# Column-tiled products, padded-query scores, merges by transfer and shift passes on GpSimd in a fused attention and MLP kernel

## The chip, the cores and the metric

The kernel runs on one core of one Trainium2 chip. The metric is the device time of one execution in microseconds (us); the number given for a kernel is the median of its runs, and lower is better. A core has TensorE (PE; its weight loads are listed apart as PEld), VectorE (DVE), ScalarE (ACT), GpSimd (POOL) and SyncE (SP), each with its own instruction queue that it works off in order. They meet through semaphores.

## The reference

```python
def reference(A_x, A_wqkv, A_wo, B_x, B_w1, B_b1, B_w2, B_b2):
    xn = _layernorm(A_x, axis=-1)            # x: [1, 2048, 448] bfloat16
    # A: attention, 16 heads of 28
    qkv = (xn @ wqkv).reshape(B, S, 3, H, Dh).transpose(2, 0, 3, 1, 4)
    scores = jnp.einsum("bhqd,bhkd->bhqk", q, k) * Dh ** -0.5
    p = _softmax(scores, axis=-1)
    s = jnp.einsum("bhqk,bhkd->bhqd", p, v).transpose(0, 2, 1, 3).reshape(B, S, D) @ wo
    # B: two dense layers, hidden width 1792
    h = _gelu(jnp.einsum("bsd,df->bsf", xn, w1) + b1)
    g = _silu(jnp.einsum("bsf,fd->bsd", h, w2) + b2)
    return A_x + s * g
```

Everything is bfloat16 on the outside; products are gathered in float32.

## The kernel before, in words

**Layout.** The 16 heads are 4 groups (g) of 4 heads; a head has a band of 32 partitions, 28 of which are its width. `qT` and `kT` hold queries and keys with the head's width on partitions, `vaug` the values with a column that gives the row sums. The 2048 queries are 4 chunks (c) of 512. A **block** is one group with one chunk, b = 4g + c, 16 in all, and a block has 64 **score tiles** of 128 keys by 512 queries for one head (16 key tiles by 4 heads): 1024 tiles in all. The last block's queries are cut into 256, 128 and 128, so that its end is short.

**Score tiles.** `t_score` (L1605) makes score tiles with matmuls of 32 rows: the four heads of a group lie in the four bands of partitions, so up to four such matmuls run side by side (row form). The result goes to the seven PSUM banks of `ring`. For most tiles ScalarE takes two (or three) banks at a time through Exp (`p_exps`, L1671) into slots `P`, which spill into idle parts of `h` and `xnT`.

**Quads.** Some key tiles are given to VectorE: four tiles of one key tile are a *quad* (`p_late`, `pick`; at most the eight key tiles of `VT` in a block). `p_apass` (L1901) turns a score bank by a scale and an offset into a 16-bit integer whose bits are an approximate exponential in bfloat16. `p_expq` (L1944) then makes two more copies of the whole quad with the integers shifted by `SH[1]` and `SH[2]` (L1960, one VectorE instruction of 128x2048 each), and the sum of the three copies, the shifted ones weighted by `VC` through `vs`, is the exponential. Under a condition (`MG`, `GQ`, `GE`) GpSimd adds the two shifted copies in four instructions of 128x512 (L1973), a *merge*; then the quad needs two products a tile instead of three. The memory for quads is a list of 23 units cut out of tensors that are idle at the time (`unit`, `unit_of`).

**Products with the values.** `t_pv` (L2033) multiplies tiles with `vaug` (or `vs`) in column form: each head writes its own 32 partitions of the PSUM bank `acc`, and four such matmuls run side by side. All other products (`t_proj` for queries and keys, `t_v` for values, `t_f1` and `p_f2` for the dense layers, `t_wo` for the output) are full 128x128 matmuls; the last 32-row pieces of some of them (`rest`) are put among score matmuls in row form.

**Normalising.** When a block is complete, `p_epi` (L2106) copies `acc` to `E_sb` (L2111, VectorE). SyncE writes the row sums to HBM (`sums`, L2117) and reads them back spread over partitions (`rs`, L2119). GpSimd raises them to the power -1 (`rc`, L2121). SyncE writes the reciprocals out (`recs`, L2123) and reads them back broadcast in four transfers (`rb`, a part of `x_sb`, L2126). GpSimd multiplies (L2130) into `qT`, whose queries are no longer needed. `t_wo` (L2140) takes these for the output of a chunk once group 3 is done, and `t_oev` forms s * g + x and stores it, for chunks 0 and 1 by an accumulating transfer from GpSimd's queue (L2166).

**What sets the order.** At build time a planner walks through the work with a clock of its own. Every piece is a `_Task` with an engine, a duration and a latency, and `start_of` (L185) says when it could start: after its inputs, after the engine's earlier work, 0.1 later where TensorE changes its form (`SWITCH`), and, for tasks marked `port`, after VectorE or GpSimd let go of what they share. `run` puts the earliest task next, within `EPS` the one of the lowest priority. What `put` (L207) has written is each engine's queue; the chip then follows it with semaphores alone. A table of knobs `BP` has a row for each block, loaded by `tune` when the scores of that block begin. `NQ` says how many picks of quads a block makes. `K.dma` books transfers with a landing time that the code assumes.

The gelu stretch lies between blocks 8 and 9: ScalarE changes its table, runs the hidden layer through Gelu, 24 of its 56 tiles straight from banks that TensorE fills at that time (`p_direct`), and changes the table back.

Of the kernel before, what the change touches and what calls it, by code (L numbers as in the profile page):

```python
# [6 lines left out]
dt = mybir.dt  # L7
ACTF = mybir.ActivationFunctionType
ALU = mybir.AluOpType
# [7 lines left out]
DH = 28  # L17
F = 1792
G = 4
C = 4  # L20
KT = 4
T = 16
FT = F // 128
# [7 lines left out]
BPN = ('S4', 'QF', 'MG', 'GQ', 'GE', 'EPS', 'HP', 'JIT', 'RM', 'RG', 'WT', 'PV0', 'PVC', 'MP', 'ND4', 'LU', 'JOINT', 'LQ', 'JMAX', 'DQ', 'URG', 'SLACK', 'UR', 'QLEAD', 'QDIST', 'R3')  # L31
BP = (
# [17 lines left out]
)  # L50
NQ = (14, 15, 11, 13, 12, 16, 14, 5, 16, 15, 16, 16, 16, 16, 14, 16)
# [10 lines left out]
MG, GQ, GE = 1, 4.0, 12  # L62
GP, MP4, GL = 4.64, 1, 1.2
# [3 lines left out]
R3 = 0  # L67
# [21 lines left out]
SEM, OWN = 0.07, 0.03  # L89
# [5 lines left out]
EA = 1  # L95
G3P = 0
# [15 lines left out]

class _Task:
    __slots__ = ("E", "fn", "reads", "writes", "dur", "lat", "rank", "w", "mode", "rows", "port")
# [5 lines left out]
    def __init__(self, E, fn, reads=(), writes=(), dur=0.1, lat=0.05, prio=5, w=1.0, mode="full", rows=(), port=False):  # L120
        self.E, self.fn, self.reads, self.writes = E, fn, list(reads), list(writes)
        self.dur, self.lat, self.rank, self.w = dur, lat, prio, w
        self.mode, self.rows, self.port = mode, set(rows), port
        if E == DVE:
            ov = min(OVERLAP, 0.4 * self.dur)
            self.dur, self.lat = self.dur - ov, self.lat + ov


class _Kernel:
    def __init__(self, nc, A_x, A_wqkv, A_wo, B_w1, B_b1, B_w2, B_b2, out):  # L130
# [12 lines left out]
        self.port = {DVE: 0.0, POOL: 0.0}  # L143
        self.procs = []
# [40 lines left out]
    def start_of(self, t):  # L185
# [5 lines left out]
        if t.port:  # L191
            s = max(s, self.port[t.E])
# [7 lines left out]
        for b in t.writes:  # L200
# [3 lines left out]
            s = max(s, b.tr + SEM)  # L204
        return s

    def put(self, t, start=None):  # L207
# [3 lines left out]
        sem = self.evsem[t.E]  # L211
        self.evcnt[t.E] += 1
# [6 lines left out]
        self.prog[t.E].append(lambda eng, f=t.fn, s=sem: f(eng).then_inc(s, 1))  # L219
        h = (sem, self.evcnt[t.E])  # L220
# [11 lines left out]
        if t.port:  # L232
            self.port[DVE if t.E == POOL else POOL] = start + t.dur
        self.tE[t.E] = max(self.tE[t.E], start + t.dur)
# [262 lines left out]
    def alloc(self):  # L497
# [16 lines left out]
        self.P = sb("P", [128, NP, 512], bf)  # L514
        self.E_sb = sb("E_sb", [128, 2, 512], bf)
# [94 lines left out]
        self.b_dum = B()  # L610
        self.b_vs = [[B() for _ in range(NS)] for _ in range(2)]
# [27 lines left out]
        self.s_x0b, self.s_wqk1 = self.sem("s_x0b"), self.sem("s_wqk1")  # L639
        self.s_out = [self.sem("s_out%d" % q) for q in range(14)]  # L640
# [1603 lines left out]
```

## Time and profile before

| | |
|---|---|
| median of 3 runs | 426.8 us (424.96 to 427.39) |
| the profiled execution | 425.0 us span |
| ScalarE | 407.8 us busy, 435 instructions |
| TensorE | 403.8 us busy, 3705 matmuls |
| VectorE | 345.9 us busy, 588 instructions |
| GpSimd | 214.2 us busy, 214 instructions |
| reciprocals on GpSimd (L2121) | 15, 3104 ns mean |
| merges on GpSimd (L1973) | 64 instructions, 1145 to 1601 ns |
| shift passes on VectorE (L1960) | 118, 676 to 1933 ns |
| accumulating transfers (L2166) | 4 of 224 KB, 4.3 us to landing |

A line of the groups gives line, engine, operation, what is written from what, the shapes and the number of instructions; then busy time in us and the mean of one in ns; then the time for which the engine stood idle just before them, and what ended it. A line of the timeline gives start, length, engine, line and operation. Matmuls overlap, so the length of a matmul is not its step: the step is read from one start to the next. A form such as 32*128 is active rows by active columns. In square brackets stands the idle time before, and its releaser.

### The profile page before, as it was taken

The page shows a single profiled execution, that of the slowest core. Times are in us where ns is not written, and L with a number is a line of the kernel's source. Part 1 is how long each engine was busy: PE and PEld are TensorE (multiplying, and loading weights), DVE is VectorE, ACT ScalarE, POOL GpSimd, SP SyncE. Part 2 cuts the span into 40 slices and gives each one's busy share as a digit, 9 for nine tenths or more (in the row PEclk, how much of TensorE's full clock was granted, in tenths as well). Part 3 has the DMA queues.
Part 4 walks back from the last instruction along what each step waited for, and adds up shares of the span by engine and source line. Part 5 has one row for each costly group of instructions (what it writes and reads, how often), then busy time and mean ns, then how long its engine had stood idle before and what let it go on. Part 6 is the DMA issues. An engine that isn't in the chain of part 4 may idle for free.

```text
span 425.0 us, 9807 instructions
## 1 busy us (share of the span) xinstructions
PE 403.8 (95%) x3705; PEld 134.1 (32%) x3705; DVE 345.9 (81%) x588; ACT 407.8 (96%) x435; POOL 214.2 (50%) x214
## 2 busy tenths in 40 slices
PE   6999999999999999999999999999999999999985
PEld 4533222333222222222223442332222233223452
DVE  8969998579989998999975127679789968899865
ACT  6999999999999999999999999999999999999983
POOL 7590330784291405406374324677599678523720
PEclk9999999999999999999999999999999999999998
DMA  8702000010000000100230100001000010206232
GB/s 259 267 3 39 2 27 2 2 26 17 27 1 27 2 25 4 29 2 2 59 122 27 26 0 2 2 3 26 2 3 25 3 28 2 69 3 113 25 73 66
DMA packets 17721, 15.31 MB, mean 36 GB/s; under 512 B 8893, under 2 KB 14761, under 8 KB 17642
## 3 DMA queue, kind: packets, MB, share of 16 engines
q1 hardware_dynamic: 16810, 13.07, 11.3%
q0 software_dynamic: 576, 0.92, 1.7%
q8 instruction: 30, 0.49, 0.5%
q10 hardware_dynamic: 288, 0.69, 0.4%
q14 instruction: 17, 0.14, 0.1%
HBM read 12.60 MB, written 2.94 MB: 37 GB/s over the span
## 4 chain that ended last, share of the span: by engine, by line
PE 66%; DVE 14%; ACT 13%; issue 5%; POOL 1%; POOLq 0%; DVEq 0%; ACTq 0%
PE ring L1617 17%; PE acc L2052 15%; PE ring L1468 9%; PE ring L1537 9%; ACT P L1671 9%; PE ring L1042 5%; ACT h L1671 3%; DVE w L1901 3%; PE ring L2140 2%; PE ring L1438 2%; PE ring L1390 2%; DVE x_sb L1960 2%; PE ring L1058 2%; DVE h L1960 1%; DVE h L1450 1%
## 5 line engine op out<-in xcount | busy, mean ns | idle before, releaser
L1671 ACT ACTIVATE P<-ring 128x1024 bf16<-128x1024 f32 (+1 forms) x262 | 259.2, 1114 | 1.5 <-PE ring L1617 1.1
L1617 PE MATMUL ring<-qT,kT 32*128 32x512 bf16 (+2 forms) x1152 | 148.6, 359 | 6.3 <-ACT P L1671 1.7
L1671 ACT ACTIVATE h<-ring 128x1024 bf16<-128x1024 f32 (+1 forms) x82 | 86.0, 1139 | 2.0 <-PE ring L1617 1.8
L1617 PEld LDWEIGHTS ring<-qT,kT 32*128 32x128 bf16 x1152 | 40.1, 91 | 121.3 <-ACT P L1671 59.8
L2121 POOL TENSOR_TENSOR rc<-rs,mone 128x16 f32<-128x16 bf16 x15 | 46.6, 3104 | 21.5 <-DMA rs<-sums 21.4
L1537 PE MATMUL ring<-w,h 128*128 128x448 bf16 x224 | 55.0, 356 | 0.6 <-ACT xnT L1671 0.5
L1468 PE MATMUL ring<-xnT,w 128*128 128x512 bf16 x201 | 54.3, 382 | 0.8 <-DVE w L1901 0.6
L2052 PE MATMUL acc<-P,vaug 128*32 128x512 bf16 (+2 forms) x627 | 52.8, 354 | 0.0
L1901 DVE TENSOR_SCALAR x_sb<-ring 128x512 uint16<-128x512 f32 x64 | 42.8, 685 | 8.4 <-PE ring L1617 8.0
L1671 ACT ACTIVATE xnT<-ring 128x1024 bf16<-128x1024 f32 (+1 forms) x34 | 35.4, 1119 | 1.6 <-PE ring L1617 1.6
L1901 DVE TENSOR_SCALAR w<-ring 128x512 uint16<-128x512 f32 x52 | 34.4, 684 | 1.0 <-PE ring L1617 0.7
L1901 DVE TENSOR_SCALAR h<-ring 128x512 uint16<-128x512 f32 x40 | 27.0, 686 | 3.7 <-PE ring L1617 3.2
L2130 POOL TENSOR_TENSOR qT<-x_sb,E_sb 128x512 bf16<-128x512 f32 x15 | 18.1, 1209 | 22.8 <-DMA x_sb<-recs 22.6
L1345 POOL TENSOR_TENSOR qsq<-qT 128x512 bf16<-128x512 bf16 x12 | 12.7, 1071 | 32.7 <-DVE qT L1339 31.4
L1468 PEld LDWEIGHTS ring<-xnT,w 128*128 128x128 bf16 x201 | 16.5, 97 | 28.0 <-issue 9.4
L2052 PE MATMUL acc<-h,vaug 128*32 128x512 bf16 x213 | 24.7, 385 | 0.3 <-DVE w L1960 0.2
L1537 PEld LDWEIGHTS ring<-w,h 128*128 128x128 bf16 x224 | 16.1, 97 | 25.8 <-issue 15.5
L1339 DVE CAST qT<-ring 128x512 bf16<-128x512 f32 x15 | 10.3, 686 | 13.2 <-PE ring L1042 13.1
L1985 POOL TENSOR_SCALAR vs<-vaug 128x128 bf16<-128x128 bf16 x32 | 10.2, 320 | 21.0 <-PE acc L2052 10.7
L2052 PEld LDWEIGHTS acc<-P,vaug 128*32 128x32 bf16 x627 | 13.9, 95 | 16.7 <-issue 13.7
L2140 PE MATMUL ring<-wo,qT 128*128 128x448 bf16 x64 | 17.0, 386 | 2.3 <-POOL qT L2130 1.5
L1450 DVE TENSOR_SCALAR h<-ring,b1c 128x512 bf16<-128x512 f32 x23 | 17.0, 744 | 2.4 <-PE ring L1438 1.2
(232 smaller groups left out, 657.0 us busy)
## 6 DMA issues: line engine op xcount, KB each, us to landing
x_sb<-recs SPq DMA_DIRECT2D x60, 64.0 KB, 2.0
w<-in_B_w_dram SPq DMA_DIRECT2D x1, 1568.0 KB, 7.7
w<-in_B_w_dram SPq DMA_DIRECT2D x1, 1344.0 KB, 8.5
x_sb<-in_A_x_dram SPq DMA_DIRECT2D x2, 448.0 KB, 5.6
out_dram<-in_A_x_dram SPq DMA_DIRECT2D x2, 448.0 KB, 10.0
out_dram<-h POOLq DMA_DIRECT2D x4, 224.0 KB, 4.3
out_dram<-h SPq DMA_DIRECT2D x8, 112.0 KB, 1.7
h<-in_A_wqkv_dram SPq DMA_DIRECT2D x3, 168.0 KB, 5.2
```

The lines of the kernel that those rows point to most:

```text
L1042: return eng.matmul(bank, w[:, k, g * 128:(g + 1) * 128], K.xnT[:, k, c * 512:(c + 1) * 512], start=(k == 0), stop=(k > 0), skip_group_che ...
L1450: yield _Task(DVE, lambda eng: eng.tensor_scalar(dst, bank, K.b1c[:, ft:ft + 1], None, op0=ALU.add), [tok, K.b_b1c], wr, 0.69, 0.0, 2)
L1468: return eng.matmul(bank, K.w1[:, k, ft * 128:(ft + 1) * 128], K.xnT[:, k, c * 512:(c + 1) * 512], start=(k == 0), stop=(k > 0), skip_grou ...
L1537: ins = eng.matmul(ps, hv[:, ft, t * 128:(t + 1) * 128], K.w2[:, ft, :], start=(ft == 0), stop=(ft == FT - 1))
L1617: return eng.matmul(dst, K.kT[32 * j:32 * j + 32, g, t * 128:(t + 1) * 128], K.qT[32 * j:32 * j + 32, g, c * 512 + q0:c * 512 + q0 + nq], ...
L1671: return eng.activation(reg[:, i0:i0 + n, :], src, ACTF.Exp, scale=SM_SCALE)
L1901: yield _Task(DVE, lambda eng: eng.tensor_scalar(K.part(u, k).bitcast(dt.uint16), K.like(u, bank), SM_SCALE * LOG2E * 128.0, (127.0 - EXP_ ...
L1960: yield _Task(DVE, lambda eng, W=W, T=T, i=i: eng.tensor_scalar(W.bitcast(u16), T.bitcast(u16), float(SH[i]), None, op0=ALU.add), bT, bW, ...
L2052: return eng.matmul(K.acc[32 * j:32 * j + 32, q0:q0 + nq], w, ap[:, col:col + nq] if len(ap.shape) == 2 else ap[:, col // 128:(col + nq) / ...
L2121: yield _Task(POOL, lambda eng: eng.tensor_tensor(K.rc[:, :], K.rs[:, :], K.mone[:, 0:1].to_broadcast([128, 16]), ALU.pow), [K.b_srs, K.b_ ...
L2130: yield _Task(POOL, lambda eng: eng.tensor_tensor(dst, K.rb, E, ALU.mult), [K.b_rb, tE], [K.b_onT[g][c]], 1.15, 0.05, 1, port=True)
L2140: ins = eng.matmul(ps, K.qT[:, g, c * 512 + t * 128:c * 512 + (t + 1) * 128], K.wo[:, g, :], start=(g == 0), stop=(g == G - 1))
```

## The change

Seven things change. (1) A new helper `_mm` splits a full product into four column tiles of 32 columns; the products of queries, keys, values, both dense layers and the output use it, transposes, first projections and column sums do not. (2) `p_pad` copies one head's queries of a block into `qpad`, a 128-row tensor that is zero elsewhere, and `p_alone` makes single tiles of quads with it in column form, with all 128 rows of `kT`. (3) A merge is one accumulating transfer from GpSimd's queue (512 KB within SBUF) instead of four GpSimd instructions, not for units 16 to 18 and not once the scores have reached block `TXB` = 14; there are 27 of them. (4) GpSimd waits for VectorE's last `port` instruction before one of its own if the planner has them close. (5) In the blocks where `PS` is set (9 and 11), one of the two shift passes of a quad is an int32 add on GpSimd in two halves: 12 passes. (6) From block `RV` = 11 on the reciprocals are taken on VectorE. (7) The table of knobs, which gets five more columns, and `NQ` have new values, and some times that the planner assumes are changed.

```diff
-BPN = (..., 'QLEAD', 'QDIST', 'R3')
+BPN = (..., 'QLEAD', 'QDIST', 'R3', 'CN', 'CS', 'SR', 'PS', 'PQ')
 BP = (
-    (1, 1, 1, 0.383, 11, 0.1, 1.15, -0.216, 0.326, 0.685, 1.08, 13, 3, 2.292, 5, 7, 0.135, 2, 1, 1, 17, 0.325, 0.811, 70, 16, 1),
...
+    (1, 1, 0, 0.383, 15, 0.1, 1.544, -0.216, 0.326, 0.811, 1.017, 13, 3, 2.292, 5, 7, 0.124, 4, 1, 1, 17, 0.367, 0.811, 74, 17, 1, 1, 3.0, 1, 0, 4.0),
...
-NQ = (14, 15, 11, 13, 12, 16, 14, 5, 16, 15, 16, 16, 16, 16, 14, 16)
+NQ = (14, 14, 16, 15, 11, 10, 9, 16, 13, 8, 11, 16, 13, 4, 8, 12)
...
+TXI, TXL = 0.95, 5.3
+CN, CS, SR = 1, 3.0, 1
+PS, PQ, PH, PD = 0, 4.0, 2, 2.3
+TXB = 14
+PJ = 3
...
-SEM, OWN = 0.07, 0.03
+SEM, OWN, SEMW = 0.07, 0.03, 0.15
...
+RV = 11
...
+def _mm(eng, out, w, x, start, stop):
+    ins = None
+    for q in range(0, 128, 32):
+        ins = eng.matmul(out[q:q + 32, :], w[:, q:q + 32], x, tile_position=(0, q), start=start, stop=stop, skip_group_check=True)
+    return ins
...
     def start_of(self, t):
...
         if t.port:
-            s = max(s, self.port[t.E])
+            s = max(s, self.port[t.E] + (SEM if t.E == POOL else 0.0))
...
-            s = max(s, b.tr + SEM)
+            s = max(s, b.tr + (SEMW if t.mode == "row" and t.E == PE else SEM))
...
     def put(self, t, start=None):
...
         self.deps(t.E, t.reads, t.writes)
+        if t.port and t.E == POOL and start < self.port[POOL] + 4.0:
+            self.wait(POOL, self.port_h)
+        sem, by = self.evsem[t.E], 1
+        if t.tx:
+            sem, by = self.s_tx[self.n_tx % len(self.s_tx)], 16
+            self.n_tx += 1
...
     def t_f1(self, c, ft, bank, tok, k, prio=None):
...
-            return eng.matmul(bank, K.w1[:, k, ft * 128:(ft + 1) * 128], K.xnT[:, k, c * 512:(c + 1) * 512],
-                              start=(k == 0), stop=(k > 0), skip_group_check=True)
+            return _mm(eng, bank, K.w1[:, k, ft * 128:(ft + 1) * 128], K.xnT[:, k, c * 512:(c + 1) * 512], k == 0, k > 0)
...
+    def p_pad(self):
+        K = self
+        yield _Task(POOL, lambda eng: eng.memset(K.qpad[:, :], 0.0), [], [K.b_pad], 1.1, 0.05, 2)
...
+        for b in range(1, NBLK - 1):
+            yield ("until", lambda: K.lq_end or len(K.lq) > 0 and K.sub_of(K.lq[0][0]) >= b)
...
+            sl = slice(32 * PJ, 32 * PJ + 32)
+            K.dma(SP, lambda eng, sl=sl, g=g, c=c: eng.dma_start(K.qpad[sl, :], K.qT[sl, g, 512 * c:512 * c + 512]), K.s_pad,
+                  reads=[K.b_qT[g][c]], writes=[K.b_pad], land=max(K.now, K.b_pad.tr, K.b_pad.tw) + (6.0 if b < 3 else 4.5))
+            K.pad_b = b
...
+    def p_alone(self):
...
+            bank, tok = yield ("bank", ok, lambda: CS, 1.0, "col")
+            e = find()
+            m = e[0] + PJ
+            e[2].remove(m)
...
+            yield _Task(PE, lambda eng, g=g, t=t, bank=bank: _mm(eng, bank, K.kT[:, g, 128 * t:128 * t + 128], K.qpad[:, :], True, True),
+                        [K.b_pad, K.b_kT[g][t // 4]], [tok], 0.218, 0.17, CS)
+            K.spawn(K.p_apass(e[1], e[0], PJ, bank, tok), e[0])
...
     def p_expq(self, m0, u):
...
         for i in (1, 2):
             W, T, bW = *K.pair(us[i], u), K.b_U[us[i]]
+            if PS in (i, 3) and K.tE[POOL] < K.now + PQ:
+                n = (W.shape[1] if len(W.shape) == 3 else 1024) // PH
+                for h in range(PH):
...
+                        return eng.tensor_tensor(w, x, k.to_broadcast(list(w.shape)), ALU.add)
+                    q = slice(4 // PH * h, 4 // PH * h + 4 // PH)
+                    yield _Task(POOL, fs, bT[q] + [K.b_shc], bW[q], PD / PH, 0.05, 2, port=True)
...
+                continue
             yield _Task(DVE, lambda eng, W=W, T=T, i=i: eng.tensor_scalar(W.bitcast(u16), T.bitcast(u16), float(SH[i]), None, op0=ALU.add),
                         bT, bW, 0.69, 0.0, 4, port=True)
...
-        if MG and K.next_m < 64 * (m0 // 64 + 1) - GE and K.tE[POOL] < K.now + GQ:
+        if MG and not {16, 17, 18} & set(us[1:]) and K.next_m < min(64 * (m0 // 64 + 1) - GE, 64 * TXB) and K.tE[POOL] < K.now + GQ:
             v, w = us[1:]
-            for k in range(0, 4, MP4):
...
-                yield _Task(POOL, lambda eng, W=W, X=X: eng.tensor_tensor(W, W, X, ALU.add), bs[0] + bs[1], bs[0], GP * MP4 / 4, 0.05 if k + MP4 < 4 else GL, 2, port=True)
+            W, X = K.unit[v], K.unit[w]
+            yield _Task(POOL, lambda eng: eng.dma_start(W, X, accum_op=ALU.add), K.b_U[v] + K.b_U[w], K.b_U[v], TXI, TXL, 2, tx=True)
...
     def p_epi(self, b):
...
-        yield _Task(POOL, lambda eng: eng.tensor_tensor(K.rc[:, :], K.rs[:, :], K.mone[:, 0:1].to_broadcast([128, 16]), ALU.pow),
-                    [K.b_srs, K.b_pads], [K.b_rc], 3.0, 0.05, 1)
+        if b >= RV:
+            yield _Task(DVE, lambda eng: eng.reciprocal(K.rc[:, :], K.rs[:, :]), [K.b_srs], [K.b_rc], 0.2, 0.05, 1)
+        else:
+            yield _Task(POOL, lambda eng: eng.tensor_tensor(K.rc[:, :], K.rs[:, :], K.mone[:, 0:1].to_broadcast([128, 16]), ALU.pow),
+                        [K.b_srs, K.b_pads], [K.b_rc], 3.0, 0.05, 1)
```

More of the change, by code (lines that the diff above doesn't have):

```diff
@@ L514, in alloc @@
         self.P = sb("P", [128, NP, 512], bf)
+        self.qpad = sb("qpad", [128, 512], bf)
+        self.shc = sb("shc", [128, 2], dt.int32)
         self.E_sb = sb("E_sb", [128, 2, 512], bf)
@@ L639, in alloc @@
         self.s_x0b, self.s_wqk1 = self.sem("s_x0b"), self.sem("s_wqk1")
+        self.s_tx, self.n_tx = [self.sem("s_tx%d" % q) for q in range(8)], 0
         self.s_out = [self.sem("s_out%d" % q) for q in range(14)]
@@ L1163, in f @@
                 return ins
-            return _Task(PE, f, [K.b_wqk[which][0], K.b_pads, K.b_xnT[0][k] if h else K.b_x0h[k]], [tok], 0.218, 0.17, which)
+            return _Task(PE, f, [K.b_wqk[which][0], K.b_pads, K.b_xnT[0][k] if h else K.b_x0h[k]], [tok], 0.218, 0.17, which, mode="full")
         def kproj(h):
@@ L1226, in f @@
             for _ in range(3):
-                ins = eng.matmul(K.acc[:, 0:128], K.zero[:, :], K.ident[:, :], start=False, stop=True,
-                                 skip_group_check=True)
+                ins = _mm(eng, K.acc[:, 0:128], K.zero[:, :], K.ident[:, :], False, True)
             return ins
@@ L1249, in f @@
             return ins
-        yield _Task(PE, f, K.b_wsq[g0:g1] + [K.b_pads], [tok], 0.15 * n + 0.1, 0.1, pr, 0.15)
+        yield _Task(PE, f, K.b_wsq[g0:g1] + [K.b_pads], [tok], 0.15 * n + 0.1, 0.1, pr, 0.15, mode="full")
         for b in K.b_hf[1]:
@@ L1351, in p_q @@
         bank2, tok2 = yield ("bank", lambda: K.ready([tq]), pp)
-        yield _Task(PE, lambda eng: eng.matmul(bank2, K.bsel[:, :], qs, start=True, stop=True),
+        yield _Task(PE, lambda eng: _mm(eng, bank2, K.bsel[:, :], qs, True, True),
                     [tq, K.b_bsel], [tok2], 0.216, 0.17, pp if g == 0 else 4)
@@ L1389, in f @@
                     ap = bass.AP(tensor=K.wv, offset=kt * WS + h0 * DH, ap=[[KT * WS, 128], [1, nh * DH]])
-                    ins = eng.matmul(bank[:, off:off + nh * DH], K.xnT[:, kt, t * 128:(t + 1) * 128], ap,
-                                     start=(kt == 0), stop=(kt > 0), skip_group_check=True)
+                    ins = _mm(eng, bank[:, off:off + nh * DH], K.xnT[:, kt, t * 128:(t + 1) * 128], ap, kt == 0, kt > 0)
             return ins
@@ L1536, in f @@
                 for ft in (2 * q, 2 * q + 1):
-                    ins = eng.matmul(ps, hv[:, ft, t * 128:(t + 1) * 128], K.w2[:, ft, :],
-                                     start=(ft == 0), stop=(ft == FT - 1))
+                    ins = _mm(eng, ps, hv[:, ft, t * 128:(t + 1) * 128], K.w2[:, ft, :], ft == 0, ft == FT - 1)
                 return ins
@@ L1805, in p_solo @@
                 return
-            now = lambda: len(K.lq) > 0 and K.can(K.lq[0][0], K.now) and (K.in_gelu() or K.next_m >= MTOT or K.urgent(K.lq[0][0]))
+            wide = lambda: K.tE[PE] <= K.now + 0.3 and sum(K.free_at(i) + SEM <= K.now + JOINT for i in range(len(K.banks))) >= min(SR, len(K.lq[0][2]))
+            now = lambda: len(K.lq) > 0 and K.can(K.lq[0][0], K.now) and (K.in_gelu() or K.next_m >= MTOT or K.urgent(K.lq[0][0])) and (SR < 2 or wide())
             yield ("until", lambda: now() or not K.lq)
@@ L2095, in p_norm4 @@
         bank, tok = yield ("bank", lambda: K.g_done[C - 1] and K.ready([tE]), 3)
-        yield _Task(PE, lambda eng: eng.matmul(bank[:, 0:128], K.selb[:, :], E, start=True, stop=True),
+        yield _Task(PE, lambda eng: _mm(eng, bank[:, 0:128], K.selb[:, :], E, True, True),
                     [tE, K.b_selb], [tok], 0.1, 0.12, 3)
@@ L2139, in f @@
             for g in gs:
-                ins = eng.matmul(ps, K.qT[:, g, c * 512 + t * 128:c * 512 + (t + 1) * 128], K.wo[:, g, :],
-                                 start=(g == 0), stop=(g == G - 1))
+                ins = _mm(eng, ps, K.qT[:, g, c * 512 + t * 128:c * 512 + (t + 1) * 128], K.wo[:, g, :], g == 0, g == G - 1)
             return ins
```

89 lines of the change are left out of this document (61 added, 28 removed), and 32 rows, old and new, of the table BP.

## The prediction

> **What bounds the kernel now.** I read the page first (busy shares), then the stretches of the span, the groups by line, the order of matmuls, and last the end of the timeline. The page's shares, then the busy time of each engine in four stretches (start, end, us, PE, PEld, DVE, ACT, POOL, clock, DMA):
>
> ```profile
> PE 403.8 (95%) x3705; PEld 134.1 (32%) x3705; DVE 345.9 (81%) x588; ACT 407.8 (96%) x435; POOL 214.2 (50%) x214
> ...
> 20.00:228.00 208.00, 200.66 (x1804) 59.45 (x1804) 184.97 (x300) 204.77 (x213) 90.29 (x93) 1.00 0.09 23
> 228.00:256.00 28.00, 27.82 (x144) 11.92 (x143) 5.64 (x9) 27.55 (x26) 11.64 (x9) 1.00 0.05 11
> 256.00:406.00 150.00, 147.28 (x1425) 46.43 (x1423) 126.24 (x193) 149.66 (x157) 97.82 (x77) 1.00 0.11 22
> 406.00:425.00 19.00, 12.62 (x201) 6.48 (x199) 10.69 (x25) 10.63 (x13) 1.81 (x2) 0.88 0.29 76
> ```
>
> From 20 to 406 us ScalarE is idle 4.0 of 386 us. It is the clock of the kernel, and TensorE stands right beside it. So the body gets shorter only where ScalarE gets less to do, which means more score tiles handed to VectorE. The groups by line say what that is worth:
>
> ```profile
> L1671 ACT ACTIVATE P<-ring 128x1024 bf16<-128x1024 f32 (+1 forms) x262 | 259.2, 1114 | 1.5 <-PE ring L1617 1.1
> ...
> L1671 ACT ACTIVATE h<-ring 128x1024 bf16<-128x1024 f32 (+1 forms) x82 | 86.0, 1139 | 2.0 <-PE ring L1617 1.8
> ...
> L1901 DVE TENSOR_SCALAR x_sb<-ring 128x512 uint16<-128x512 f32 x64 | 42.8, 685 | 8.4 <-PE ring L1617 8.0
> ```
>
> With the 34 into xnT, L1671 has 378 instructions, 32 of them three tiles wide: 346x2 + 32x3 = 788 of the 1024 tiles. The other 236 are L1901's on VectorE: 59 quads of four tiles. L1671 is busy 356.5 us in the four stretches, 0.4525 us a tile, so one more quad takes **1.81 us** off ScalarE.
>
> What TensorE could give back shows in its timeline (start, length, instructions):
>
> ```profile
> 345.10 0.39 PE L2052 MATMUL acc<-kT,vs 128*32 128x512 bf16 x4
> 345.43 0.39 PE L1617 MATMUL ring<-qT,kT 32*128 32x512 bf16 x3
> 345.75 0.40 PE L2052 MATMUL acc<-vaug,vs 128*32 128x512 bf16 x4
> ...
> 346.62 0.39 PE L2052 MATMUL acc<-xnT,vs 128*32 128x512 bf16 x4
> 346.84 0.39 PE L2052 MATMUL acc<-xnT,vaug 128*32 128x512 bf16 x4
> 347.16 1.31 PE L1537 MATMUL ring<-w,h 128*128 128x448 bf16 x6
> 348.40 0.40 PE L1617 MATMUL ring<-qT,kT 32*128 32x512 bf16 x4
> ```
>
> Four column tiles after four take 0.22 us (346.62 to 346.84). Where the form changes, the step is 0.32 (346.84 to 347.16, 345.43 to 345.75): 0.10 us lost at each change. I counted the changes over all matmul records in order of time: full to or from row 393, column to or from row 283, column to or from full 41.
>
> The end has a stall of its own:
>
> ```profile
> 397.43 3.66 POOL L1973 TENSOR_TENSOR xnT<-xnT,h 128x512 bf16<-128x512 bf16 x3
> 397.63 0.34 SPq L2119 DMA_DIRECT2D rs<-sums  x1
> 401.12 3.31 POOL L2121 TENSOR_TENSOR rc<-rs,mone 128x16 f32<-128x16 bf16 x1
> 406.12 1.72 SPq L2126 DMA_DIRECT2D x_sb<-recs  x4
> 410.93 1.14 POOL L2130 TENSOR_TENSOR qT<-x_sb,E_sb 128x512 bf16<-128x512 f32 x1 [4.26 <-DMA x_sb<-recs]
> 412.12 0.55 PE L2140 MATMUL ring<-wo,qT 128*128 128x448 bf16 x2 [1.54 <-POOL qT L2130]
> 413.05 1.45 ACT L1671 ACTIVATE xnT<-ring 128x1536 bf16<-128x1536 f32 x1 [1.58 <-PE ring L1617]
> 413.85 3.87 PE L2140 MATMUL ring<-wo,qT 128*128 128x448 bf16 x11
> ```
>
> Block 14's reciprocals wait for a GpSimd merge, its output products wait for them, the last scores stand behind those products, and after the stall the granted clock is 0.51 from 413.75 to 417.20: eleven products take 3.87 us.
>
> **The change, part by part.** *Column products.* Some 720 full products (224 of L1537, 201 of L1468, 106 of L1042, 124 of L1390, 64 of L2140) become four column tiles each. Successive groups of four 512-wide column tiles start 0.216 to 0.226 us apart, full ones 0.216: cost 0 to 7 us of TensorE, taken 2. The 41 changes between column and full go: 41 x 0.10 = 4.1 back. Row changes stay, so most of the 717 do. Against this stands the Trainium skill, TensorEngine Tiling (Array Packing), Performance Considerations: each matmul has some 60 cycles of overhead, so a tiling factor should not be bought with more instructions. By it the sum would grow by three overheads a product; the trace disagrees for tiles that run side by side, since groups of four 128-wide column tiles start 0.055 us apart, as single full 128-wide ones do.
>
> *Padded-query scores.* No row shows one. It streams 512 columns, 0.218 us for one tile, but needs no visit to row form. 63 row starts carry one tile alone. If each were a visit of its own, 63 x 0.2 = 12.6 us come back; if each shared its visit, or the padded tile could have ridden free in a row group, it loses up to 63 x 0.22. The bounds are far apart; I take +5, since a schedule with a choice uses it mostly where the visit is saved. The 14 copies of qT into qpad cost SyncE about 0.34 us each (L2119's issue), 4.8 us. Behind them in its queue stand the sums, rs, recs and rb transfers; these feed L2130, which only the output products of the last four blocks read. Cover gone, as for block 14, one costs its 0.34 and a landing of 2 us.
>
> *Merges.* L1973 has 64 instructions, 16 quads, 4.6 us each: 75 us leave GpSimd, and 27 issues at the 0.9 us of L2166 (24 us) come. TensorE saves 4 matmuls for each of 11 more merges: 11 x 0.226 = 2.5 us. Their landing has no row: 512 KB in SBUF, while L2166 accumulates 224 KB in 4.1 to 5.5 us and plain 448 KB loads land in 4.2 to 5.6. Plain loads scaled by size give 4.8 to 6.4; a line through L2163 (112 KB, 1.7) and L2166 (224 KB, 4.3) gives 11. The code reckons 0.95 + 5.3 = 6.25. I take 6.3, as size and partitions are nearest the loads. Behind a late merge stands all of TensorE.
>
> *GpSimd waits and int32 adds.* 14 of L1960's 118 shift passes take 0.95 to 1.93 us where the rest take 0.68; the excess over all is 11 us. The new wait is on GpSimd, before its port instructions, and holds vs, rb products and silu products up by at most one pass; GpSimd is half idle, which covers it. It can stop only the half in which VectorE comes first: VectorE gains 0 to 11, taken 5.5. The 12 passes moved free 12 x 0.685 = 8.2 us more and give GpSimd 24 halves; L1973's 1.15 us for 512 elements is the nearest row, 28 us. Four reciprocals come to VectorE: L2099 takes 0.96 for 128 columns, so 16 columns lie between 0.12 and 0.96, taken 0.2. Behind each wait L1901 passes and the banks; rs is in 3.2 us after the cast (block 14: 396.0 to 397.63 + 1.6), so with the reckoned 4.4 us for it the wait is over; if rs took its longest, 3.4, it would cost 1.8 us, once in four.
>
> *What it buys.* TensorE is freed by 4.1 - 2 + 5 + 2.5 = 9.6 us. A further quad shortens the body by 1.81, which TensorE must do without, and adds 0.23 (merged) to 0.45 of products, less 0.2 to 0.4 for fewer changes: about 1.75. That is 5.5 quads. VectorE is freed by 13; a quad asks 4 x 0.685 + 2 x 0.69 + 1.81 = 5.9, so 2.2 quads, more if part of its 47 idle us (outside the stretch from 228) is used. Between these: 4 quads, **-7.2 us**; bounds 0 and 8 (-14.5).
>
> *The end.* rs had landed at 399.2; the reciprocal runs then instead of ending at 404.4, and no merge is left in blocks 14 and 15. 4.4 us earlier removes the 1.58 us of ScalarE and the half clock (11 x 0.18 = 2.0): 3.6 at most, 0 if another chain is right behind; taken **-3.0**.
>
> Sum on the profile's own 425.0: 414.8. That span equals the lowest of the runs (424.96); the median lies 1.8 higher, so **416.6**.
>
> **Rivals.** *More room than I count* (0.20): idle time of TensorE (some 35 us in the body by the same records) is used too, 8 quads and 3.6 at the end: 425 - 18.1 + 1.8 = 408.7. For it: VectorE's 47 idle us. Against: it is already near 90% busy up to 228.
>
> *Nothing converts* (0.12): padded scores lose what column form gains, VectorE fills first, and only 0 to 3 us at the end come: 423.8 to 426.8. For it: the 2.2 quads of VectorE.
>
> *Merges land late* (0.15, slower). TensorE takes its queue in order, and products of blocks come in turns of eight tiles, 8 x 788/1024 x 0.4525 = 2.8 us, so a merge has 1.4 us of slack on the mean. At 8.7 us, halfway from 6.4 to 11, each of 27 stops TensorE for 8.7 - 6.25 - 1.4 = 1.05 us: 28 us, 444 in all. It decides from about 8.0 us, where 27 x 0.38 eats the 10.2. For it: a GpSimd issue at 384.29 took 1.41 us, with a shift pass beside it, the others 0.9. Against: the plain loads. The Trainium skill, SBUF - State Buffer, "SBUF: two separate sides", says just that: VectorE in a two-port mode keeps GpSimd from writing descriptors; that one issue agrees.
>
> *The column form doesn't run side by side for products* (0.03): each of three more tiles costs the 0.025 us at which the one-column products of L1247 follow one another: 720 x 0.075 = 54, 470 us. Against: L2052's groups.
>
> **How the numbers follow.** The forecast has 0.50, with 412 to 421 of its own (2 to 6 quads, 2 to 3.6 us). Within 0.5% means 424.7 to 428.9, about what runs of this kernel can tell from no change. Faster: 0.50 + 0.20 + 0.05 of the third = 0.75; same 0.06; slower 0.19. The range runs from 406 to 429 and leaves out the late merges, the last rival and a little below.
>
> **What would show it.** L1901 about 252 times and L1671's tiles 16 fewer; groups of four column tiles 0.22 us apart in L1537 and L1468; few or no changes between full and column; rc from VectorE within 1 us of rs; clock 1.0 up to the last products. Wrong if L1901 stays at 236, if TensorE waits for the POOL queue's merges for more than 5 us in all, or if VectorE's waits for rs add up.

## The result and the profile after

The changed kernel takes **432.44 us** (median of 4 runs, 431.06 to 434.23), the kernel before 427.1 in the same comparison: a ratio of **1.0148** (95% interval 1.0109 to 1.0187). It is slower by 1.5%, where 416.6 was forecast. The profiled execution has a span of 430.3 us against 425.0.

The page of the changed kernel, busy shares and then two rows of the 40 slices (ScalarE's busy share and the granted clock, 10.8 us a slice):

```profile
PE 403.2 (94%) x6226; PEld 146.0 (34%) x6226; DVE 345.3 (80%) x598; ACT 403.6 (94%) x418; POOL 175.6 (41%) x200
...
ACT  5898299999999999999999999999999999989993
...
PEclk9999599999999999999999999999999999999999
```

ScalarE has 4.2 us less to do than before (407.8), GpSimd 39 less, and still the span is 5.3 longer. What the slices show is one hole: in the fifth, from 43 to 54 us, ScalarE is busy for a fifth of the time and the granted clock is half. After it ScalarE is full up to the end.

The groups by line (columns as in the prediction):

```profile
L1696 ACT ACTIVATE P<-ring 128x1024 bf16<-128x1024 f32 (+1 forms) x239 | 249.0, 1127 | 13.0 <-PE ring L1642 11.8
...
L1975 DVE TENSOR_SCALAR vaug<-ring 128x512 uint16<-128x512 f32 x84 | 56.0, 685 | 8.6 <-PE ring L1642 6.5
...
L122 PE MATMUL ring<-qpad,kT 128*32 128x512 bf16 x140 | 14.3, 405 | 6.3 <-DMA qpad<-qT 6.2
```

Over all its groups L1975 (before: L1901) has 248 instructions instead of 236, and the exponentials (L1696) make 776 tiles instead of 788: three more quads, 62 for 59. But the exponentials into `P` wait 13.0 us for score banks instead of 1.5, and the last line says where that begins: the padded-query tiles wait once, 6.2 us, for the copy of queries into `qpad`. The timeline around that place, SyncE's queue (SPq, whose length is the time until the last of its issues) with ScalarE and the waiting matmuls:

```profile
33.62 7.87 SPq L907 DMA_DIRECT2D wo<-in_A_wo_dram  x16
41.53 0.25 SPq L838 DMA_DIRECT2D w<-in_B_b_dram  x1
41.82 0.39 SPq L840 DMA_DIRECT2D b1h<-in_B_b_dram  x1
42.26 1.72 SPq L907 DMA_DIRECT2D out_dram<-in_A_x_dram  x2
42.37 1.03 ACT L1696 ACTIVATE P<-ring 128x1024 bf16<-128x1024 f32 x1
44.02 0.59 SPq L1869 DMA_DIRECT2D qpad<-qT  x1
48.25 0.62 PE L122 MATMUL ring<-qpad,kT 128*32 128x512 bf16 x4 [6.22 <-DMA qpad<-qT]
50.73 1.02 ACT L1696 ACTIVATE P<-ring 128x1024 bf16<-128x1024 f32 x1 [7.32 <-PE ring L1642]
```

The first copy into `qpad`, that of block 1, is 32 KB. SyncE issues it only when it has issued 16 transfers of `wo`, two of the biases and two copies of x; it is issued at 44.02 and lands at 48.2. TensorE takes its queue in order, so everything behind the first padded tile stands, and ScalarE is without a bank for 7.32 us. The busy times from 43 to 55 us (columns as in the prediction), the changed kernel and then the kernel before:

```profile
43.00:55.00 12.00, 6.75 (x56) 1.48 (x60) 3.93 (x7) 3.65 (x5) 0.20 (x1) 0.57 0.32 79
```

```profile
43.00:55.00 12.00, 11.51 (x112) 3.21 (x110) 11.10 (x19) 11.93 (x14) 5.51 (x9) 1.00 0.01 2
```

ScalarE loses 8.3 of these 12 us, partly because the granted clock is still at half when TensorE gets going again (0.57 on the mean of this stretch). The transfers that stood ahead were in the trace before as well, in SyncE's part of the timeline, but the two copies of x were out of the way there at 9.69 us, and `wo` began 2.1 us earlier:

```profile
9.69 1.36 SPq L877 DMA_DIRECT2D out_dram<-in_A_x_dram  x2
...
31.54 6.77 SPq L877 DMA_DIRECT2D wo<-in_A_wo_dram  x16
38.36 0.25 SPq L808 DMA_DIRECT2D w<-in_B_b_dram  x1
38.65 0.40 SPq L810 DMA_DIRECT2D b1h<-in_B_b_dram  x1
```

The transfers of `wo` waited for GpSimd there too (its memset of `wo`), but nothing that TensorE needs soon stood behind them.

### The profile page after: what moved, and what is told of

Read it like the earlier page. It is cut to its first block, busy times and chain, and to the rows that moved or that the text cites. A ratio compares the mean times of both kernels' runs of the same rounds, so it can differ in the third digit from the quotient of the medians.

```text
span 430.3 us, 14825 instructions
## 1 busy us (share of the span) xinstructions
PE 403.2 (94%) x6226; PEld 146.0 (34%) x6226; DVE 345.3 (80%) x598; ACT 403.6 (94%) x418; POOL 175.6 (41%) x200
## 4 chain that ended last, share of the span: by engine, by line
PE 63%; DVE 13%; ACT 9%; DMA 6%; issue 6%; POOL 1%; SPq 1%; DVEq 0%; POOLq 0%; ACTq 0%
PE ring L122 30%; PE ring L1642 17%; PE acc L2133 13%; ACT P L1696 6%; ACT h L1696 2%; DMA h<-kT 2%; DMA x_sb<-x_sb 2%; DVE st L981 1%; DVE vaug L1975 1%; DVE w L1975 1%; ACT xnT L1696 1%; PE ring L1465 1%; DMA qpad<-qT 1%; DVE x_sb L1975 1%; DVE kT L2048 1%
## 5 line engine op out<-in xcount | busy, mean ns | idle before, releaser
L1696 ACT ACTIVATE P<-ring 128x1024 bf16<-128x1024 f32 (+1 forms) x239 | 249.0, 1127 | 13.0 <-PE ring L1642 11.8
L1696 ACT ACTIVATE h<-ring 128x1024 bf16<-128x1024 f32 (+1 forms) x82 | 86.4, 1116 | 1.6 <-PE ring L1642 1.4
L1642 PEld LDWEIGHTS ring<-qT,kT 32*128 32x128 bf16 x1117 | 37.4, 91 | 124.6 <-ACT P L1696 54.6
L1975 DVE TENSOR_SCALAR vaug<-ring 128x512 uint16<-128x512 f32 x84 | 56.0, 685 | 8.6 <-PE ring L1642 6.5
L122 PE MATMUL ring<-xnT,w 128*32 128x512 bf16 x852 | 57.9, 381 | 0.1
L122 PE MATMUL ring<-w,h 128*32 128x448 bf16 x896 | 56.4, 355 | 0.1
L1696 ACT ACTIVATE xnT<-ring 128x1024 bf16<-128x1024 f32 (+1 forms) x42 | 41.8, 1049 | 0.7 <-PE acc L2133 0.4
L2205 POOL TENSOR_TENSOR rc<-rs,mone 128x16 f32<-128x16 bf16 x11 | 34.2, 3110 | 15.3 <-DMA rs<-sums 15.2
L1975 DVE TENSOR_SCALAR w<-ring 128x512 uint16<-128x512 f32 x32 | 21.6, 686 | 11.5 <-PE ring L122 8.3
L1975 DVE TENSOR_SCALAR x_sb<-ring 128x512 uint16<-128x512 f32 x44 | 29.0, 684 | 1.6 <-PE ring L1642 1.2
L122 PEld LDWEIGHTS ring<-xnT,w 128*32 128x32 bf16 x852 | 20.7, 96 | 24.9 <-issue 7.9
L1975 DVE TENSOR_SCALAR h<-ring 128x512 uint16<-128x512 f32 x32 | 21.3, 683 | 5.5 <-PE ring L1642 5.5
L122 PEld LDWEIGHTS ring<-w,h 128*32 128x32 bf16 x896 | 18.1, 95 | 22.4 <-issue 13.3
L122 PE MATMUL ring<-qpad,kT 128*32 128x512 bf16 x140 | 14.3, 405 | 6.3 <-DMA qpad<-qT 6.2
L122 PE MATMUL ring<-wo,qT 128*32 128x448 bf16 x256 | 16.0, 355 | 2.6 <-DVE qT L2183 1.5
```

The source lines that it names most:

```text
L122: ins = eng.matmul(out[q:q + 32, :], w[:, q:q + 32], x, tile_position=(0, q), start=start, stop=stop, skip_group_check=True)
L1642: return eng.matmul(dst, K.kT[32 * j:32 * j + 32, g, t * 128:(t + 1) * 128], K.qT[32 * j:32 * j + 32, g, c * 512 + q0:c * 512 + q0 + nq], ...
L1696: return eng.activation(reg[:, i0:i0 + n, :], src, ACTF.Exp, scale=SM_SCALE)
L1975: yield _Task(DVE, lambda eng: eng.tensor_scalar(K.part(u, k).bitcast(dt.uint16), K.like(u, bank), SM_SCALE * LOG2E * 128.0, (127.0 - EXP_ ...
L2205: yield _Task(POOL, lambda eng: eng.tensor_tensor(K.rc[:, :], K.rs[:, :], K.mone[:, 0:1].to_broadcast([128, 16]), ALU.pow), [K.b_srs, K.b_ ...
```

## The experiments

Each kernel is the changed one with the edit shown; ratios are to the kernel before on the same chip. e3, e5, e6, e7 and e8 contain the edit of e1, and are read against e1. e5 to e8 were timed on another chip than e1, where the kernel before took 426.5 us instead of 425.9; of these, e8 differs from e1 by the place of the x copies alone (423.85 us), so that the losses of e5, e6 and e7 are given against e8 as well.

**e1: block 1's copy from another queue.** The order of work on TensorE, ScalarE and VectorE stays as it is.

```diff
-            K.dma(SP, lambda eng, ...: eng.dma_start(K.qpad[sl, :], K.qT[sl, g, 512 * c:512 * c + 512]), K.s_pad,
+            K.dma(ACT if b == 1 else SP, lambda eng, ...: eng.dma_start(K.qpad[sl, :], K.qT[sl, g, 512 * c:512 * c + 512]), K.s_pad,
```

> One word of the changed kernel is altered: block 1's copy into qpad is issued from ScalarE's queue, not from SyncE's, where it stands behind the 16 transfers of wo, the two of b1 and the two 448 KB copies of x. Every other queue has the same order. Theory (the copy's place in SyncE's queue costs the time): it lands before 42 us, TensorE does not wait 6.2 us at 42.0, ScalarE does not stand idle 7.3 us, the clock does not halve; the span falls from 430.3 to 421 to 423. Rival (the landing itself is slow, 4.2 us where 1.8 is usual, or the blocks 0 and 1 are too tight in any case): a wait of 3 us or more stays, span 425 or more.

Measured: 422.85 us, ratio **0.9925** (0.9892 to 0.9959), span 420.0. That is faster than both kernels. Its page and timeline:

```profile
PE 401.0 (95%) x6226; PEld 146.8 (35%) x6226; DVE 344.4 (82%) x598; ACT 402.8 (96%) x418; POOL 174.9 (42%) x200
```

```profile
34.46 0.59 ACTq L1869 DMA_DIRECT2D qpad<-qT  x1
41.51 0.40 PE L122 MATMUL ring<-qpad,kT 128*32 128x512 bf16 x4
```

The copy is issued at 34.46, 9.6 us earlier, lands in 3.4 us and is first used at 41.51, with no wait. One transfer's place in a queue was worth some 9.5 us (a ratio of 1.0148 against 0.9925). ScalarE's time outside its work is 17.2 us now (420.0 less 402.8) and was 17.2 before (425.0 less 407.8): the gain of 5.0 us in span over the kernel before is the 5.0 us that ScalarE has less to do. That holds for these two executions. The one of e1 is the shortest of its eight; by the medians of one chip the gain is 3.0 us (425.85 against 422.85).

**e2: the two copies of x ahead of `wo` in SyncE's queue**, so that two issues fewer stand ahead of the copy, which stays on SyncE.

```diff
-            yield ("until", lambda: K.late_on)
+            yield ("until", lambda: True)
```

> Only SyncE's order differs from the changed kernel: the two 448 KB copies of x to the output are issued ahead of the wo transfers, as in the kernel before, so that block 1's qpad copy stands behind wo and b1 alone. If the copies of x are in its way by 1.7 us of issue and 2.4 us of a slower landing, it is issued at 42.3 and lands at 44.2, the wait falls from 6.2 to about 2 us, and the span to about 425.5. If only its place behind the wo transfers counts, or the landing is slow for another reason, the wait stays at 4 us or more and the span at 428 or more.

Measured: 429.01 us, ratio 1.0077 (1.0044 to 1.0109), span 427.5. Timeline:

```profile
41.53 0.85 SPq L1869 DMA_DIRECT2D qpad<-qT  x1
...
45.83 0.62 PE L122 MATMUL ring<-qpad,kT 128*32 128x512 bf16 x4 [4.37 <-DMA qpad<-qT]
```

The issue comes 2.5 us earlier, as meant, but the landing is still 4.3 us, where the other 13 copies take a median of 1.8. So half of the expectation held: the x copies delay the issue, and something other than them makes the landing slow.

**e9: as e2, with the load of `b1h` on ScalarE's queue.** The load is 3.5 KB in single elements of two bytes, and it stood directly ahead of the copy.

```diff
-            K.dma(SP, lambda eng: eng.dma_start(K.b1h[:, :], K.B_b1.rearrange("(f p) -> p f", p=128), ...), K.s_b1h,
+            K.dma(ACT, lambda eng: eng.dma_start(K.b1h[:, :], K.B_b1.rearrange("(f p) -> p f", p=128), ...), K.s_b1h,
```

> As the run with the copies of x ahead of the wo transfers (block 1's qpad copy still on SyncE's queue, behind wo), but the load of b1h, 3.5 KB in pieces of 2 bytes, which stood directly ahead of the qpad copy, is issued from ScalarE's queue some 10 us earlier. The order of work is the same. Theory (the qpad copy's landing was 4.3 us since it came in behind the pieces of b1h): issued at 41.2, landed at 43.1, a wait of 1 to 2 us on TensorE instead of 4.4, span 422.5 to 424. Rival (the landing is slow behind the wo transfers): the landing stays near 4 us, the wait near 4, span 426 or more.

Measured: 428.85 us, ratio 1.0068 (1.0035 to 1.0102), span 425.9. Timeline:

```profile
41.62 0.57 SPq L1869 DMA_DIRECT2D qpad<-qT  x1
...
44.87 0.60 PE L122 MATMUL ring<-qpad,kT 128*32 128x512 bf16 x4 [3.26 <-DMA qpad<-qT]
```

The landing falls from 4.3 to 3.2 us: `b1h` explains 1.1 us of it. The landing lies between the two theories, the span next to the rival's 426. The transfers of `wo` are still in flight on the same queue at that time (their last packets end at 42.4 us in the trace), but the order in the queue is not the whole rest. The copy's own packets run from 1.2 to 2.3 us after its issue, where those of an undisturbed copy run from 1.2 to 1.5, and the landing comes another 1.0 us later, where 0.3 is usual. What holds it after its last packet stays open. Over the four kernels ScalarE's idle time at this place and the span go together: 7.32 and 430.3, 5.36 and 427.5 (e2), 4.22 and 425.9 (e9), none and 420.0 (e1).

**e8: e1 and e2 together.**

> Block 1's qpad copy on ScalarE's queue, and the two copies of x to the output ahead of the wo transfers on SyncE's. Theory (only the copy's own place cost time): the same as with the copy on ScalarE's queue alone, within 0.3%. Rival (the copies of x in the stretch from 42 us disturb other loads): 0.5 to 1.5 us faster.

Measured: 423.85 us, ratio 0.9938 (0.9913 to 0.9962), no different from e1 beyond the noise. Once the copy has left SyncE's queue, the place of the x copies is worth nothing.

**e4: no padded tiles in block 1**, with the whole order of work worked out anew (58 quads, 22 merges).

```diff
-        for b in range(1, NBLK - 1):
+        for b in range(2, NBLK - 1):
```

> The changed kernel with no qpad copy for block 1 (the loop starts at block 2), so that block 1's tiles of quads are all scored in row form; the order of all work is derived anew and has 58 quads in place of 62, 22 merges in place of 27. Theory (the early wait is gone, a quad is worth 1.81 us of ScalarE): 430.3 - 8.5 + 4 x 1.81 = 429 us of span. Rival (the number of quads does not set the time): about 422.

Measured: 434.86 us, ratio 1.0192 (1.0126 to 1.0258), span 432.2, slower than expected. ScalarE is busy 410.1 us, 7.3 more than in e1, about what the four quads that it lacks are worth (4 x 1.81); the other 4.9 us of span between the two are idle time of ScalarE. The same fault shows in another place (timeline):

```profile
205.21 0.41 SPq L907 DMA_DIRECT2D w<-in_B_w_dram  x1
205.72 0.91 SPq L1869 DMA_DIRECT2D qpad<-qT  x1
...
213.83 0.40 PE L122 MATMUL ring<-qpad,kT 128*32 128x512 bf16 x4 [2.65 <-DMA qpad<-qT]
```

Here the copy is issued at once, but behind a load of 1568 KB: it lands after 8.1 us, and TensorE waits 2.65.

**e3: e1 with full products.**

```diff
-    ins = None
-    for q in range(0, 128, 32):
-        ins = eng.matmul(out[q:q + 32, :], w[:, q:q + 32], x, tile_position=(0, q), start=start, stop=stop, skip_group_check=True)
-    return ins
+    return eng.matmul(out, w, x, start=start, stop=stop, skip_group_check=True)
```

> As the run with the qpad copy on ScalarE's queue, but the helper for products issues one full 128x128 matmul in place of four column tiles, in the same order of tasks. In the changed kernel's trace products or padded tiles stand next to products with the values 83 times without a change of form; each would now cost 0.10 us: 8.3 us more for TensorE. Theory (TensorE is as tight as ScalarE): 4 to 8 us slower than that run. Rival (ScalarE is the bound and TensorE has room): less than 1 us slower. If full matmuls are cheaper than column tiles by 0.01 us each, as I had allowed for, 7 us of it come back.

Measured: 428.13 us, ratio 1.0052 (1.0019 to 1.0085), 5.3 us more than e1. Its page:

```profile
PE 409.3 (96%) x3694; PEld 138.0 (32%) x3694; DVE 343.9 (80%) x598; ACT 404.7 (94%) x418; POOL 175.5 (41%) x200
```

TensorE is busy 8.3 us longer, which is the 83 x 0.10 of the expectation, but only by luck. The exponentials that begin at 399.40 us in e1 begin at 403.36 in e3: 4.0 us of span and 5.4 us of TensorE's busy time lie ahead of that point. The other 4.6 us of span and the rest of the busy time come at the end, where TensorE waits for GpSimd in e3 and the granted clock is then half from 408.4 to 415.3 us, which it is not in e1 (1.06 us of waiting at this place):

```profile
408.49 0.93 PE L120 MATMUL ring<-wo,qT 128*128 128x448 bf16 x2 [2.72 <-POOL qT L2211]
```

By the matmul records e3 changes the form 756 times and e1 672 times, so a change saved is worth 0.06 us of TensorE here and not 0.10. The step of the column form costs nothing: groups of four start 0.216 us apart at 512 columns, as full matmuls do. But a row group starts 0.009 us later behind a column product than behind a full one (medians of 0.321 against 0.312 us at 512 columns, of 0.294 against 0.285 at 448); over the 174 places where e3 has a full product ahead of a row group that is some 1.6 us. So the column form is worth about 4 us of time in the body.

**e5: e1 without GpSimd's wait for VectorE's last port instruction.**

```diff
-        if t.port and t.E == POOL and start < self.port[POOL] + 4.0:
-            self.wait(POOL, self.port_h)
```

> The kernel with block 1's qpad copy on ScalarE's queue, without the new wait of GpSimd for VectorE's last port instruction; the order of work is the same. Theory (the wait is what keeps shift passes short): of the 112 shift passes on VectorE some 12 instead of 4 take over 0.8 us, 5 to 8 us more of VectorE, and the time rises by 0 to 3 us. Rival (passes got short because the merges left GpSimd): still 4 to 6 long passes and the same time within 1 us.

Measured: 429.41 us, ratio 1.0054 (1.002 to 1.0088), 6.6 more than e1 and 5.6 more than e8, where 0 to 3 was expected. Timeline of e5, shift passes (VectorE) and silu products (GpSimd), then the exponential that follows:

```profile
368.08 1.36 POOL L1583 TENSOR_TENSOR h<-h,w 128x448 bf16<-128x448 bf16 x1
368.47 1.52 DVE L2046 TENSOR_SCALAR kT<-xnT 128x2048 uint16<-128x2048 uint16 x1
369.52 1.36 POOL L1581 TENSOR_TENSOR h<-w 128x448 bf16<-128x448 bf16 x1
369.92 1.52 DVE L2046 TENSOR_SCALAR x_sb<-xnT 128x2048 uint16<-128x2048 uint16 x1
...
374.05 1.02 ACT L1694 ACTIVATE P<-ring 128x1024 bf16<-128x1024 f32 x1 [2.73 <-PE ring L1640]
```

and e1 at the same work:

```profile
366.25 1.52 DVE L2048 TENSOR_SCALAR kT<-xnT 128x2048 uint16<-128x2048 uint16 x1
367.70 0.68 DVE L2048 TENSOR_SCALAR x_sb<-xnT 128x2048 uint16<-128x2048 uint16 x1
...
369.13 1.03 POOL L1583 TENSOR_TENSOR h<-w 128x448 bf16<-128x448 bf16 x1 [1.91 <-DVE kT L2048]
```

Side by side a shift pass takes 1.52 us and a product 1.36; one after the other they take 0.68 and 1.03. In e5 13 passes are over 0.8 us, in e1 4; the passes take 85.5 us in all against 79.6. A run of slow passes holds the banks, and ScalarE with them: e5's exponentials are 2.2 us behind those of e1 ahead of the place shown and 5.1 behind it, where the granted clock is half from 374.2 to 377.6 us. The other 3.4 of the 6.3 us of span I did not follow place by place, so it is not shown that each us that VectorE loses is one of time.

**e6: e1 with the reciprocals of blocks 11 to 14 on GpSimd (power -1).**

```diff
-            yield _Task(DVE, lambda eng: eng.reciprocal(K.rc[:, :], K.rs[:, :]), [K.b_srs], [K.b_rc], 0.2, 0.05, 1)
+            t = _Task(DVE, lambda eng: eng.tensor_tensor(K.rc[:, :], K.rs[:, :], K.mone[:, 0:1].to_broadcast([128, 16]), ALU.pow),
+                      [K.b_srs], [K.b_rc], 0.2, 0.05, 1)
+            t.on = POOL
+            yield t
```

> The kernel with block 1's qpad copy on ScalarE's queue, with the reciprocals of blocks 11 to 14 as GpSimd's power again; the order of work is otherwise the same. Theory (block 14's chain sets the end): rc ends 2 to 3 us later, the output products and the last scores behind them wait as long, 1.5 to 3 us slower. Rival (the end is set by the scores, not by this chain): no difference beyond 1 us; VectorE's queue even loses 4 x 0.24 us.

Measured: 429.12 us, ratio 1.0068 (1.0036 to 1.0099), 6.3 more than e1 and 5.3 more than e8. Timeline of e6 and then of e1:

```profile
395.33 3.63 POOL L2204 TENSOR_TENSOR rc<-rs,mone 128x16 f32<-128x16 bf16 x1
...
406.69 0.56 PE L122 MATMUL ring<-wo,qT 128*32 128x448 bf16 x8 [3.57 <-POOL qT L2218]
```

```profile
394.20 0.25 DVE L2203 RECIPROCAL rc<-rs 128x16 f32<-128x16 bf16 x1
...
402.87 0.56 PE L122 MATMUL ring<-wo,qT 128*32 128x448 bf16 x8 [1.06 <-POOL qT L2214]
```

The reciprocal of block 14 takes 3.4 us longer and the output products wait 2.5 us longer; 1.5 to 3 was expected. Of the 5.2 us of span only 1.3 come ahead of this place: the exponentials that begin at 399.40 us in e1 begin at 400.71 in e6. The end adds 4.0, and after the longer wait the granted clock is half from 408.1 to 411.5 us. In e8, whose reciprocals are those of e1, the clock is half there too (405.0 to 408.4), and the end takes 1.9 us longer than in e1. So up to half of what the end adds can be the clock, and the reciprocals are its cause only in part.

**e7: e1 with each merge in four GpSimd instructions** on the same order of work.

```diff
-            yield _Task(POOL, lambda eng: eng.dma_start(W, X, accum_op=ALU.add), K.b_U[v] + K.b_U[w], K.b_U[v], TXI, TXL, 2, tx=True)
+            def fm(eng):
+                ins = None
+                for k in range(4):
+                    x, y = W[:, 512 * k:512 * k + 512], X[:, 512 * k:512 * k + 512]
+                    ins = eng.tensor_tensor(x, x, y, ALU.add)
+                return ins
...
+            yield t
```

> The kernel with block 1's qpad copy on ScalarE's queue, with each of the 27 merges made by four GpSimd instructions of 128x512 where the transfer was issued; the order of work is otherwise the same, and its assumed times are those of a transfer. Theory (a transfer lands in 4.6 to 5.9 us, four instructions take 4.6 us, so products find their input about as early; but GpSimd is busy 100 us longer and holds the port): more long shift passes, 5 to 15 us more of VectorE, queues behind GpSimd late, 3 to 10 us slower. Rival (GpSimd has the room): within 1 us.

Measured: 462.61 us, ratio 1.0839 (1.0785 to 1.0893), 40 more than e1 (39 more than e8), four times what was expected at most. Its page:

```profile
PE 411.9 (89%) x6226; PEld 146.9 (32%) x6226; DVE 363.7 (79%) x598; ACT 406.6 (88%) x418; POOL 287.7 (62%) x281
```

GpSimd is busy 112.8 us longer and VectorE 19.3, the price of 108 instructions on the port that they share; the exponentials into `P` wait 32.2 us for banks. This says that this order can't be run without the transfers, not that they are worth 40 us: the kernel before had another order around 16 merges on GpSimd.

The padded tiles were not taken out by themselves: that changes the whole order of work, as in e4.

## Why the prediction was wrong, by its own steps

**The step that failed** is the one on the copies: "The 14 copies of qT into qpad cost SyncE about 0.34 us each (L2119's issue), 4.8 us. Behind them in its queue stand the sums, rs, recs and rb transfers". I asked what stands behind the copies, and not what stands ahead of the first one and who waits for it. Ahead of it stand 16 transfers of `wo`, and behind the wait stands all of TensorE: a wait of 6.2 us, which the prediction had at nothing and which puts the exponentials behind it 9.3 us behind those of e1. That the place was tight was to be had: SyncE was in the transfers of `wo` up to 38.3 us and in those of the biases up to 39.05, so that a copy behind them would land at about 41 with the usual 1.8 us, or at 42.2 with the 3.2 of e9, and a padded tile of block 1 is due at 41.5 (e1). The stall itself could not be read there, since `wo` began 2.1 us later in the changed kernel and the x copies came to stand ahead as well. The sentence "Cover gone, as for block 14, one costs its 0.34 and a landing of 2 us" had the right shape and was priced only for the sums. None of the rivals named this either: the late-merge rival had the right mechanism, TensorE in order behind a transfer, on the wrong transfer.

The last step of the sum, 1.8 us from the span to the median, came out right by luck. The prediction took the profiled execution for the run of 424.96 us, since its span was 425.0. But a time is 1.8 us above the span of its own execution (432.1 and 430.3 for the changed kernel), so the profiled one was that of 426.8 us, which was the median itself.

The other terms can be read in e1, where this stall is gone. Its span of 420.0 stands against the 414.8 of the sum, and its median of 422.85 against 416.6:

| term | predicted | what the runs showed |
|---|---|---|
| more quads | 4, -7.2 us | 3; ScalarE has 4.0 us less to do between its first and last exponential, 5.0 in all (e1) |
| column products cost TensorE | 2 us | step 0.216 us, as before; some 1.6 us at the changes to row form (e1, e3) |
| form changes saved | 41, 4.1 us | 717 fell to 672; undoing the form adds 84, 5.4 us of TensorE ahead of the end (e3) |
| GpSimd's port waits, for VectorE | 5.5 us | 5.9 us (e5), 5.6 to 6.6 of time |
| 12 passes moved, on GpSimd | 28 us | 25.1 us, 24 halves of 1.03 to 1.41 (e1) |
| reciprocal on VectorE | 0.2 us | 0.24 to 0.25 us |
| merges' landing | 6.3 us | 4.5 to 8.0 us, median 5.1 |
| issue of a copy into `qpad` | 0.34 us | 0.56 us, median |
| the end | -3.0 us | -3.2 us (e1), -1.4 (e8) |

*Quads.* The direction was right, and the number was three. The price of 1.81 us was a little low: it divides the 356.5 us from 20 us on by all 788 tiles, and with the 7.2 us of exponentials ahead of 20 us it is 1.85. Where the fourth went can't be told from these runs; VectorE stood at 82% in e1, so its full queue alone doesn't show it. Padded scores (+5) have no run of their own, and stay open.

*Merges.* Three groups of them among the transfers of the changed kernel (KB each, median us from issue to landing):

```profile
w<-x_sb POOLq DMA_DIRECT2D x3, 512.0 KB, 5.2
x_sb<-h POOLq DMA_DIRECT2D x3, 512.0 KB, 5.7
...
h<-qsq POOLq DMA_DIRECT2D x1, 512.0 KB, 8.0
```

Scaling from the plain loads (4.8 to 6.4) was right, the line through the two small accumulating transfers (11) was not. Four merges take 7.2 us or longer, and TensorE's matmuls wait for two of the 27, by 0.4 us together; the slack of 1.4 us was enough. The late-merge rival is out.

*Column form.* The rule of the Trainium skill, TensorEngine Tiling (Array Packing), Performance Considerations, that each matmul brings some 60 cycles was weighed in the prediction against the trace. The trace decides: 2532 more matmuls (6226 against 3694) go with 5.4 us less of TensorE in e1 than in e3, up to the same exponentials and at the full granted clock. For tiles that run side by side this overhead doesn't show.

*The end.* From the last exponential to the end it was 9.2 us (425.0 less 415.85), in e1 7.0 (420.0 less 412.98). In the 20 us up to that point ScalarE was idle for 1.8 us, in e1 for 0.8. Together that is 3.2 us, and 3.0 stood in the sum. The way there was longer than reckoned: the reciprocal of block 14 runs 5.1 us after the block's cast (394.20 against 389.08) instead of the 3.2 at which rs was reckoned in. SyncE issues rs 2.4 us after the cast, not 1.6, and when it is due (391.44 + 1.6 = 393.0) VectorE still has a shift pass and an output step ahead of the reciprocal. ScalarE keeps a wait of 0.66 us before its last tiles, where 1.58 stood. In e8, where the granted clock is half from 405.0 to 408.4 us, ScalarE is idle for 2.7 us there and the end gives 1.4, so that the 3.2 of e1 is a good execution and not a rule.

The sum was thus 5.2 us too good without the stall: 3.2 of the quads (4.0 us instead of 7.2), 0.6 at the start (the first exponential runs at 13.3 us instead of 12.8), and 1.6 of waits of ScalarE in the body, which add up to 5.4 us instead of 3.8 (the longest are 1.14 us ahead of 37.48 and 1.04 ahead of 370.16, both for TensorE), less the 0.2 that the end gave more.

## What to carry to other kernels

A transfer that is added to a queue has two neighbours: price what stands behind it and also what stands ahead of it at the moment when its first user is due, and take its landing from copies in that company, not from copies that travel alone. If its user is an engine that works in order and bounds the kernel, a 32 KB copy can cost more than all the rest of a change brings; here another queue mended it. In an order that is fitted tightly, taking a single part out cost 5 to 7 us each time (e3, e5, e6), together far more than the 3 us that the whole change gains without the stall, so such parts can't be added up. And a busy time that matches an estimate to the tenth (e3) is to be read stretch by stretch before it is believed.

## What the runs showed of the hardware that I had not expected

- The landing of the same 32 KB copy within SBUF: a median of 1.8 us over SyncE's copies, 3.2 behind the transfers of `wo` (e9), 4.2 to 4.3 with `b1h` ahead as well, 8.1 behind a load of 1568 KB (e4). On ScalarE's queue, while `wo` was on SyncE's, it took 3.4 (e1). The Trainium skill, DMA: Bandwidth & Descriptors, Queues, rings and completion order, says that a DMA engine takes the descriptors of one ring in order and goes round between the rings of different queues, packet by packet. The copies behind x (changed kernel) and behind the load (e4) fit that: their first packets run 2.6 and 5.5 us after the issue, where 1.2 is usual. The 1.0 to 1.7 us between the last packet and the landing in e9 and e2 (0.3 is usual) are not explained by it.
- In the traces the granted clock, once it was half in the course of a kernel, stayed so for 3.4, 6.8 or 10.2 us: 10.2 after a wait of TensorE of 6.2 us (44.3 to 54.6 us), 6.8 after waits of 4.4 (e2) and 2.7 (e3), 3.4 after waits of 1.4 (e8), 1.5 (kernel before), 2.7 (e4), 3.3 (e9) and 3.6 us (e6); after the 1.1 us of e1 at the place of e8 it did not fall. So the stall of one engine went on after its cause was gone: in the changed kernel TensorE was back at 48.25 us.
- VectorE's shift passes and GpSimd's products slow each other both: from 0.68 to 1.52 us and from 1.03 to 1.36 us (e5).
